# Closing rows of q from sums on VectorE and two matmuls, q's first tiles at tile 12, three modulation sums at tiles 11 to 15

## The chip, the core and the metric

The kernel runs on one core of one Trainium2 chip. The metric is the device time of one execution in microseconds (us). Five engines work beside each other: TensorE (PE in the profile, its weight loads PEld), VectorE (DVE), ScalarE (ACT), GpSimd (POOL) and SyncE (SP), which here only issues loads and stores. Each runs its own queue of instructions in the order in which the program issues them and waits on semaphores for the others.

## What is computed

The reference is a transformer block with adaptive layer norm, for 2048 tokens of width 448, all float32:

```python
mod = (_silu(c) @ w_mod).reshape(c.shape[0], 6, 1, -1)
sa, ca, ga, sb, cb, gb = (mod[:, 0], mod[:, 1], mod[:, 2], mod[:, 3], mod[:, 4], mod[:, 5])
h = _layernorm(x, axis=-1) * (1 + ca) + sa
x = x + ga * _A_ref(h, A_wqkv, A_wo)
h = _layernorm(x, axis=-1) * (1 + cb) + sb
x = x + gb * _B_ref(h, B_w1, B_b1, B_w2, B_b2)
```

`_A_ref` is linear attention with 16 heads of 28: q, k, v are `h @ wqkv`; q and k go through phi(t) = t + 1 for t > 0, else exp(t), plus 1e-6; `kv` and `z` are sums over all tokens of phi(k) v and phi(k); the output is (phi(q) kv) / (phi(q) z) times `wo`. `_B_ref` is an MLP across the tokens (2048 to 1792 and back, with GELU).

## The kernel before

Tokens are cut into 16 tiles of 128 (`NT`), channels into 4 chunks (three of 128 and one of 64). A float32 product is built from a rounded high part and a low remainder, so that one product takes three matmuls (high-high, high-low, low-high). A matmul with 448 columns is the unit of PE's work nearly everywhere.

The order of all instructions is written out by hand. The part around the change is the loop over tiles `t = 4 .. 15` (L674 to L765). One turn issues, in this order:

- **PE**: `project(t+1)`, ten matmuls of k for the next tile; `close(t)`, one matmul that adds the layer norm's mean and bias to k through "closing rows" (`Wrow`); `a_outer(t-4)`, eleven matmuls that add the tile's phi(k) times x to four banks; at odd t `a_transpose(t+1)`, which turns the means and deviations of tiles t+1 and t+2 into rows that `close` needs; and, where `Q_EARLY` says so, `a_q(i)`, the ten matmuls and the closing one of q for tile i.
- **ACT**: exponentials and ReLUs of q from the turn before (`a_exp_q`, two per tile of q); at odd t `a_copy(t+1)`, `a_copy(t+2)`, which put the transposed rows into the operand that `close` loads; `a_exp(t)` for k (at t = 9 ahead of the copies); `a_split_high(t+3)`; `a_pk_parts(t-1)`; `a_high(t-2)`.
- **DVE**: at odd t `bn_stats` of x for tiles t+3 and t+4 (the first at the start of the turn, the second late in it); `phi_q`; `a_norm`; `a_pk(t)`; `a_split_low(t+3)`; `a_low`; then at the end of the turn the sums of modulation vectors (`mod_part(j, i)`, one of four steps for vector j).
- **POOL**: the power of the variances (`a_pow`) and two accumulating DMAs per tile (`a_pk_parts`, L524, and `sum_end`, L538).
- **SP**: loads of later tiles (`FETCH`), of modulation weights (`load_mod(j)`, four loads of 196 KB) and others. Each waits for a free buffer of the pool `slots` (74 buffers of 128 x 512 float32).

Two places carry the change:

- The **closing rows of q**, `Wrow[0]`. q's weights are scaled by 1 + ca on ACT (`w_high`, tiles 4 to 7) and DVE (`w_low`, tiles 5 to 8). The rows hold minus the sum of the scaled weights over the channels and the product with sa. At t = 9, between `close(9)` and `a_outer(5)`, PE builds both: `row_sum(0)` (L290, seven matmuls of a selecting matrix `sel_s` with the high and low weights) and `row_bias(0)` (L296, one float32 matmul with `accb`, which DVE summed in `row_part`, tiles 5 to 8). `row_out(0)` (L299) rounds them into `Wrow[0]` on ACT and DVE at the end of t = 9. Tiles 0 to 4 of q follow at t = 10 to 14; the other eleven come after the loop.
- The **modulation vectors** 2 (ga), 4 (1 + cb) and 3 (sb): loaded by `load_mod`, summed in four steps on DVE, split by `mod_split`, summed over partitions by a matmul with ones (`mod_sum2`), and copied out by `mod_out`. ga multiplies the four pieces of `wo` (L764, L776).

After the loop come the last phi(k) parts, the sum `pksum`, its split `zs`, the last outer products, `zp` (L784, two matmuls of `zs` with ones), `zb` (L786), splits of the MLP's weights (`split_to`), `csum` (L795, L796) and `kvb` (L805), which PE multiplies from `csum` and v's weights.

Of the kernel before, what the change touches and what calls it, by code (L numbers as in the profile page):

```python
# [8 lines left out]
F32 = mybir.dt.float32  # L9
F32R = mybir.dt.float32r  # L10
AF = mybir.ActivationFunctionType
ALU = mybir.AluOpType
# [15 lines left out]
Q_EARLY = {10: 0, 11: 1, 12: 2, 13: 3, 14: 4}  # L28
RING = 3
FETCH = {4: 11, 5: 12, 7: 13, 9: 14, 10: 15}  # L30
# [9 lines left out]
MOD_AT = {9: [(4, 0)], 10: [(4, 1)], 11: [(4, 2)], 12: [(4, 3)], 13: [(3, 0)], 14: [(3, 1)]}  # L40
# [12 lines left out]
def block_kernel(ctx: ExitStack, tc: tile.TileContext, x, xt, wqkv, wo, w1, b1, w2, b2, c, wmod, wfirst, out):  # L53
# [63 lines left out]
    sel_s = cst.tile([P, ROWS], F32R, name="sel_s")  # L117
    rowst = []
# [19 lines left out]
    def load_mod(j):  # L138
        for k in range(4):
            wm[j, k] = (tslot if j == 5 else slot)(f"wm{j}_{k}", parts=G)  # L140
            nc.sync.dma_start(wm[j, k], wmod[k * G:(k + 1) * G, j * D:(j + 1) * D])
# [148 lines left out]
    def row_sum(j):  # L290
        rowb[j] = bank(f"rowb{j}")
        ws = [Whi[j, ch] for ch in range(4)] + [Wlo[j, ch] for ch in range(3)]
        for i, w in enumerate(ws):
            nc.tensor.matmul(rowb[j][:ROWS, :D], sel_s, w, start=(i == 0), stop=False)

    def row_bias(j):  # L296
        nc.tensor.matmul(rowb[j][:ROWS, :D], sel_b, accb.pop(j), start=False, stop=True)

# [180 lines left out]
    def a_q(t):  # L479
        project(t, 0, "qp")  # L480
        qps[t] = close(t, 0)
        del heads[t]
# [138 lines left out]
    load_mod(2)  # L621
# [51 lines left out]
    late = [t for t in range(NT) if t not in Q_EARLY.values()]  # L673
    for t in range(4, NT):  # L674
# [3 lines left out]
        if t == 9:  # L678
            row_sum(0)
            row_bias(0)  # L680
# [4 lines left out]
        if t in Q_EARLY:  # L685
            a_q(Q_EARLY[t])
        if t == 12:
            mp = mod_sum2(2)
# [10 lines left out]
        a_phi_q(t in Q_EARLY)  # L699
        if t == 9:  # L700
            a_exp(t, kp)
# [3 lines left out]
        if t != 9:  # L705
            a_exp(t, kp)
# [29 lines left out]
        if t == 9:  # L736
            row_out(0)
        if t == 12:
            mod_out(2, mp)
            make_mask()  # L740
# [3 lines left out]
        if 7 <= t < 11:  # L744
            mod_part(2, t - 7)
        if t == 11:
            mod_split(2)
        for j, i in MOD_AT.get(t, ()):
            mod_part(j, i)
        if t in (7, 10):  # L750
            load_mod(4 if t == 7 else 3)
# [11 lines left out]
        if t >= 13:  # L763
            nc.vector.tensor_mul(wo_sb[t - 13], wo_sb[t - 13], mods[2][:G])  # L764
# [11 lines left out]
    nc.vector.tensor_mul(wo_sb[3], wo_sb[3], mods[2][:G])  # L776
# [587 lines left out]
```

## Time and profile before

| what | us |
|---|---|
| median of 3 runs (lowest, highest) | 436.17 (435.62, 436.36) |
| the profiled execution | 435.4 |
| its span in the profile | 433.7 |
| the granted clock of PE, all 40 slices | 0.9 or more of full speed |

The profile is one execution on the chip. Times in it count from the span's start. A view named "timeline" lists instructions of an engine: start, duration, engine, line, operation, output and inputs, and in brackets the idle time before it with what ended it. The "chain of waits" follows the last instruction back to what released it, step by step, so that its rows together fill the span. The "waits" list who waited for whom: total, times, longest. Successive matmuls overlap: a 448-column matmul lasts 0.36 us in the list, and the next one starts about 0.20 us after it, so PE's cost is read from starts.

### The profile page before, as it was taken

How to read it: one execution, taken by the hardware profiler on the slowest of the kernel's cores; microseconds unless marked ns; L12 is line 12 of the kernel's file. 1: busy time of each engine (PE TensorE's matmuls, PEld its weight loads, DVE VectorE, ACT ScalarE, POOL GpSimd, SP SyncE). 2: the span in 40 equal slices, each digit the busy share in tenths (PEclk: the TensorE clock that was granted, in tenths of full speed). 3: DMA queues.
4: the chain of work that ended last, by engine and by line, in shares of the span. 5: the costliest groups of instructions: out<-in, count | busy, mean ns of one | idle time of the engine just before them, and what ended most of it. 6: DMA issues, size and time to landing. Idle time of an engine off the chain costs nothing.

```text
span 433.7 us, 7208 instructions
## 1 busy us (share of the span) xinstructions
PE 428.1 (99%) x2333; PEld 395.5 (91%) x2333; DVE 362.2 (84%) x813; ACT 278.5 (64%) x595; POOL 119.6 (28%) x198
## 2 busy tenths in 40 slices
PE   8999999999999999999999999999999999999996
PEld 7788899999899989989999999999999999999996
DVE  4999987689799999996579695739799998898893
ACT  5899868658578799985855263537464664645550
POOL 2336444300025577775200000010113131122010
PEclk9999999999999999999999999999999999999999
DMA  8998996574200036345427461587479977886430
GB/s 278 384 334 179 242 249 152 107 225 164 86 1 0 26 73 148 73 98 121 147 85 241 144 212 50 167 209 201 85 181 215 228 157 153 218 176 125 82 54 32
DMA packets 63941, 66.14 MB, mean 152 GB/s; under 512 B 4960, under 2 KB 55456, under 8 KB 63904
## 3 DMA queue, kind: packets, MB, share of 16 engines
q1 hardware_dynamic: 54832, 50.90, 37.8%
q0 software_dynamic: 8784, 14.32, 21.1%
q10 hardware_dynamic: 288, 0.46, 0.5%
q8 instruction: 18, 0.29, 0.3%
q14 instruction: 19, 0.16, 0.1%
HBM read 46.30 MB, written 7.34 MB: 124 GB/s over the span
## 4 chain that ended last, share of the span: by engine, by line
PE 92%; DVE 4%; DMA 2%; issue 0%; POOL 0%; ACT 0%; SPq 0%; DVEq 0%
PE y L1159 19%; PE up L939 10%; PE up L938 10%; PE up L940 10%; PE y L1160 9%; PE cacc L551 8%; PE qp L439 7%; PE op L881 6%; PE kp L439 5%; PE tq L851 1%; PE op L888 1%; DMA wr<-in_qkv_dram 1%; DMA xt<-in_xt_dram 1%; PE qp L446 1%; PE kvb L805 1%; PE wp L955 1%
## 5 line engine op out<-in xcount | busy, mean ns | idle before, releaser
L939 PE MATMUL up<-h2l,ph 128*128 128x448 f32 x224 | 81.3, 363 | 0.0
L938 PE MATMUL up<-h2h,ph 128*128 128x448 f32 x224 | 81.2, 362 | 0.0
L940 PE MATMUL up<-h2h,pl 128*128 128x448 f32 x224 | 80.8, 361 | 0.0
L1114 POOL DMA_DIRECT2D a<-a x16 | 14.2, 962 | 137.8 <-DMA a<-in_B_w_dram 77.6
L938 PEld LDWEIGHTS up<-h2h,ph 128*128 128x128 f32 x224 | 42.0, 188 | 3.2
L940 PEld LDWEIGHTS up<-h2h,pl 128*128 128x128 f32 x224 | 41.9, 187 | 3.0
L939 PEld LDWEIGHTS up<-h2l,ph 128*128 128x128 f32 x224 | 42.0, 188 | 2.6 <-DVE h2l L935 0.3
L85 DVE TENSOR_TENSOR pl<-pr,ph 128x512 fp32r<-128x512 f32 x46 | 30.8, 688 | 4.1 <-ACT ph L84 3.3
L1165 ACT ACTIVATE cc<-y 128x448 f32<-128x448 f32 x24 | 13.0, 546 | 26.8 <-PE y L1160 26.8
L84 ACT ACTIVATE ph<-pr 128x512 fp32r<-128x512 f32 x46 | 27.6, 623 | 0.8 <-PE up L940 0.5
L1078 DVE TENSOR_TENSOR u<-u,mod 128x448 f32<-128x448 f32 x14 | 8.7, 623 | 21.7 <-ACT u L1077 21.5
L1077 ACT ACTIVATE u<-up,b1c 128x448 f32<-128x448 f32 x14 | 8.8, 625 | 24.1 <-PE up L940 23.5
L1179 POOL DMA_DIRECT2D out_dram<-yt x14 | 12.7, 908 | 40.8 <-DVE yt L1170 31.4
L439 PE MATMUL kp<-wh,hh 128*128 128x448 f32 x64 | 23.7, 375 | 0.0
L551 PE MATMUL cacc<-pkh,xh 128*128 128x448 f32 x64 | 23.6, 369 | 0.0
L439 PE MATMUL qp<-wh,hh 128*128 128x448 f32 x64 | 23.4, 366 | 0.0
L831 POOL TENSOR_SCALAR den<-den 128x16 f32<-128x16 f32 x16 | 8.8, 549 | 45.4 <-DVE den L828 45.4
L551 PE MATMUL cacc<-pkl,xh 128*128 128x448 f32 x56 | 20.3, 362 | 0.0
L881 PE MATMUL op<-wph,pth 128*128 128x448 f32 x48 | 18.7, 390 | 0.0
L1120 DVE TENSOR_TENSOR a<-a,s 128x512 f32<-128x512 f32 (+1 forms) x32 | 18.5, 622 | 0.0
L84 ACT ACTIVATE s2h<-s 128x512 fp32r<-128x512 f32 (+1 forms) x16 | 8.3, 569 | 15.5 <-DVE s L1120 15.5
L1159 PE MATMUL y<-ub,a11h 128*128 128x448 f32 x56 | 18.2, 375 | 0.0
(239 smaller groups left out, 1378.1 us busy)
## 6 DMA issues: line engine op xcount, KB each, us to landing
pr<-in_B_w_dram SPq DMA_DIRECT2D x56, 256.0 KB, 3.1
a<-in_B_w_dram SPq DMA_DIRECT2D x32, 256.0 KB, 4.4
a<-in_B_w_dram SPq DMA_DIRECT2D x32, 192.0 KB, 4.2
xt<-in_xt_dram SPq DMA_DIRECT2D x16, 256.0 KB, 5.0
x<-in_A_x_dram SPq DMA_DIRECT2D x16, 224.0 KB, 5.0
wm<-in_B_wmod_dram SPq DMA_DIRECT2D x16, 196.0 KB, 5.4
out_dram<-x SPq DMA_DIRECT2D x14, 224.0 KB, 2.2
out_dram<-yt POOLq DMA_DIRECT2D x14, 224.0 KB, 5.7
```

The source lines that it names most:

```text
L84: nc.scalar.activation(hi, full, AF.Copy)
L85: nc.vector.tensor_sub(lo, full, hi.bitcast(F32))
L439: nc.tensor.matmul(pps[t, j][:, :D], a[:, ch * P:(ch + 1) * P], w, start=first, stop=False)
L551: nc.tensor.matmul(cacc[ch][:, :D], a[:, s], b, start=(t == 0 and i == 0), stop=(t == NT - 1 and i == len(todo) - 1))
L881: nc.tensor.matmul(opb[t][:, :D], a, b, start=(ch == n == 0), stop=False)
L938: nc.tensor.matmul(ps[:, :D], hi[:, sl], mh, start=first, stop=False)
L939: nc.tensor.matmul(ps[:, :D], hi[:, sl], ml, start=False, stop=False)
L940: nc.tensor.matmul(ps[:, :D], lo[:, sl], mh, start=False, stop=last)
L1114: nc.gpsimd.dma_start(w, a, accum_op=ALU.add)
L1120: nc.vector.tensor_tensor(w, raw2[q, a][i], raw2[q, b][i], op=op)
L1159: nc.tensor.matmul(ps[:, :D], h[:, s], w, start=opens and r == 0, stop=False, skip_group_check=True)
L1160: nc.tensor.matmul(ps[:, :HD], l[:, s], wh, start=False, stop=closes and r == PAIRS - 1, skip_group_check=True)
```

## The change

q's closing rows are no longer built by eight matmuls at t = 9. DVE sums the scaled weights over the four chunks into one tile `accs` (`row_main`: chunks 0 and 1 at t = 9, chunks 2 and 3 at t = 10). `row_fold` (end of t = 10) adds the two halves of the partitions, of this sum and of `accb`, into the two halves of one tile. `row_cut` (t = 11, ahead of the turn's copies) splits it, on ACT and DVE. `row_both` (t = 12, after `close(12)`) multiplies the high and low part with a new selecting matrix `sel_q`, two matmuls, and `row_out(0)` follows at once. `sel_q` is made by `make_sel_q` at the end of t = 8: seven memsets on POOL and a rounding copy on ACT.

Tiles 0 to 4 of q move from t = 10 .. 14 to t = 12 (two), 13, 14 and 15. The first loads of modulation weights move from ahead of the loop to t = 7 (vector 2), and from t = 7 and 10 to t = 9 (4) and 11 (3). The sums move from t = 7 .. 14 to t = 11 .. 15; the split of vector 2 from t = 11 to 13, its matmul and copy (and the mask's memset) from t = 12 to 14; the products of `wo` from t = 13, 14, 15 and one after the loop to two at t = 15 and two after it. At t = 9, `a_exp` goes behind the copies as at other odd tiles.

```diff
-Q_EARLY = {10: 0, 11: 1, 12: 2, 13: 3, 14: 4}
+Q_EARLY = {12: (0, 1), 13: (2,), 14: (3,), 15: (4,)}
+ROW_AT = 12
+MAIN_AT = {9: (0, 1), 10: (2, 3)}
+MOD2_AT = {11: (0,), 12: (1, 2, 3)}
 RING = 3
+LOAD_MOD = {7: 2, 9: 4, 11: 3}
...
-MOD_AT = {9: [(4, 0)], 10: [(4, 1)], 11: [(4, 2)], 12: [(4, 3)], 13: [(3, 0)], 14: [(3, 1)]}
+MOD_AT = {13: [(4, 0), (4, 1)], 14: [(4, 2), (4, 3)], 15: [(3, 0), (3, 1)]}
...
+    def make_sel_q():
+        g = slot("sel_g", P)
+        nc.gpsimd.memset(g, 0.0)
+        for i in (64, 66, 96):
+            nc.gpsimd.memset(g[:64, i:i + 1], -1.0)
+            nc.gpsimd.memset(g[64:, i + 1:i + 2], 1.0)
+        nc.scalar.activation(sel_q, g, AF.Copy)
+
+    def row_main(j, ch):
+        p = slice(0, P) if ch < 3 else slice(0, 64)
+        if ch == 0:
+            accs[j] = slot(f"accs{j}")
+            nc.vector.tensor_scalar_mul(accs[j], raw_w[j, 0], col[1][:, 0:1])
+        else:
+            nc.vector.scalar_tensor_tensor(accs[j][p], raw_w[j, ch][p], col[1][p, ch:ch + 1], accs[j][p],
+                                           op0=ALU.mult, op1=ALU.add)
+
+    def row_fold(j):
+        s, b = accs[j], accb.pop(j)
+        nc.vector.tensor_add(s[:64], s[:64], s[64:])
+        nc.vector.tensor_add(s[64:], b[64:], b[:64])
+
+    def row_cut(j):
+        s = accs.pop(j)
+        hi, lo = moving(slot, f"rfh{j}"), moving(slot, f"rfl{j}")
+        nc.scalar.activation(hi, s, AF.Copy)
+        nc.vector.tensor_sub(lo, s, hi.bitcast(F32))
+        accs[j] = (hi, lo)
+
+    def row_both(j):
+        rowb[j] = bank(f"rowb{j}")
+        for i, m in enumerate(accs.pop(j)):
+            nc.tensor.matmul(rowb[j][:ROWS, :D], sel_q[:, :ROWS], m, start=(i == 0), stop=(i == 1))
...
-    load_mod(2)
...
-        if t == 9:
-            row_sum(0)
-            row_bias(0)
+        if t == ROW_AT:
+            row_both(0)
+            row_out(0)
...
-        if t in Q_EARLY:
-            a_q(Q_EARLY[t])
-        if t == 12:
+        for i in Q_EARLY.get(t, ()):
+            a_q(i)
+        if t == 14:
             mp = mod_sum2(2)
...
-        a_phi_q(t in Q_EARLY)
-        if t == 9:
-            a_exp(t, kp)
+        a_phi_q(len(Q_EARLY.get(t, ())))
+        if t == ROW_AT - 1:
+            row_cut(0)
...
-        if t != 9:
-            a_exp(t, kp)
+        a_exp(t, kp)
...
-        if t == 9:
-            row_out(0)
-        if t == 12:
+        for ch in MAIN_AT.get(t, ()):
+            row_main(0, ch)
+        if t == ROW_AT - 2:
+            row_fold(0)
+        if t == 8:
+            make_sel_q()
+        if t == 14:
             mod_out(2, mp)
             make_mask()
...
-        if 7 <= t < 11:
-            mod_part(2, t - 7)
-        if t == 11:
+        for i in MOD2_AT.get(t, ()):
+            mod_part(2, i)
+        if t == 13:
             mod_split(2)
...
-        if t in (7, 10):
-            load_mod(4 if t == 7 else 3)
+        if t in LOAD_MOD:
+            load_mod(LOAD_MOD[t])
...
-        if t >= 13:
-            nc.vector.tensor_mul(wo_sb[t - 13], wo_sb[t - 13], mods[2][:G])
+        if t == 15:
+            for w in wo_sb[:2]:
+                nc.vector.tensor_mul(w, w, mods[2][:G])
...
-    nc.vector.tensor_mul(wo_sb[3], wo_sb[3], mods[2][:G])
+    for w in wo_sb[2:]:
+        nc.vector.tensor_mul(w, w, mods[2][:G])
```

More of the change, by code (lines that the diff above doesn't have):

```diff
@@ L117, in block_kernel @@
     sel_s = cst.tile([P, ROWS], F32R, name="sel_s")
+    sel_q = cst.tile([P, P], F32R, name="sel_q")
     rowst = []
@@ L297, in row_bias @@
         nc.tensor.matmul(rowb[j][:ROWS, :D], sel_b, accb.pop(j), start=False, stop=True)
+    accs = {}
+    def make_sel_q():
[27 more added lines that the diff above has]
+            nc.tensor.matmul(rowb[j][:ROWS, :D], sel_q[:, :ROWS], m, start=(i == 0), stop=(i == 1))
     def row_out(j):
@@ L672, in block_kernel @@
     wo_sb = []
-    late = [t for t in range(NT) if t not in Q_EARLY.values()]
+    late = [t for t in range(NT) if t not in sum(Q_EARLY.values(), ())]
     for t in range(4, NT):
```

## The prediction

> **What bounds the kernel now.** I read the page's first part, then the windows, then the chain of waits around t = 9, then the timelines of the queues there.
>
> ```profile
> PE 428.1 (99%) x2333; PEld 395.5 (91%) x2333; DVE 362.2 (84%) x813; ACT 278.5 (64%) x595; POOL 119.6 (28%) x198
> ```
>
> ```profile
> 40.00:50.00 10.00, 10.00 (x51) 8.87 (x50) 9.82 (x26) 9.84 (x21) 6.12 (x7) 1.00 0.99 208
> ...
> 60.00:70.00 10.00, 10.00 (x53) 9.31 (x52) 7.09 (x17) 4.85 (x11) 3.05 (x4) 1.00 1.01 258
> ```
>
> PE is busy nearly the whole span, at full clock (1.00 in the windows), so a matmul less is time less, and a stall of PE is time more. But DVE and ACT (9.82 and 9.84 of 10 us) are as full as PE between 40 and 50 us, and have room only from 60 us on (7.09 and 4.85), where q's tiles stretch each turn on PE.
>
> ```profile
> 48.50 1.42 PE rowb L294 x7
> 49.92 0.75 PE rowb L297 x2
> 50.67 2.21 PE cacc L551 x11
> ...
> 57.41 2.00 PE qp L439 x10
> ```
>
> In the chain (start, us, what) the matmuls of the closing rows stand on PE from 48.50 to 50.67, with nothing beside them. Ten matmuls take 2.00 us, so one takes 0.20. A turn without q takes 2.00 + 0.20 + 2.21 = 4.41 us, a tile of q adds 2.20.
>
> **The change part by part.**
>
> *PE.* The chain loses 2.17 us (48.50 to 50.67) and gains two matmuls, 0.41: **-1.76 us**. q's matmuls only move. Bounds: -1.76, and -1.0 if only the seven matmuls' 1.42 were saved and the float32 matmul's stretch came back as another gap. I take the whole stretch, since the chain shows it as PE's own time.
>
> *Turns 9 to 12.* When PE would need things without a stall: from 48.50, `a_outer(5)` and the transposition 2.32, turn 10 4.41, turn 11 4.52, `project(13)` and `close(12)` 2.20, the two new matmuls 0.41, `a_outer(8)` 2.21, `project` of q's tile 0 2.00, so its closing matmul, which needs the new rows, is due at 66.6. `close(10)` is due at 52.8, `close(12)` at 61.8. Turns 10 and 11 lose q's 2.20 each: DVE and ACT lose that room. First comes the new wait, for `sel_q`. ACT and POOL as they stand:
>
> ```profile
> 50.08 0.62 ACT L453 ACTIVATE ek<-kp,mv 128x448 f32<-128x448 f32 x1
> 50.60 0.63 ACT L456 ACTIVATE rk<-kp,mv 128x448 f32<-128x448 f32 x1
> 53.03 0.57 ACT L414 ACTIVATE hl<-rw 34x128 fp32r<-34x128 f32 x2 [1.81 <-PE rw L411]
> ```
>
> ```profile
> 50.11 0.86 POOL L524 DMA_DIRECT2D pkl<-pk  x1 [0.47 <-ACT pkl L523]
> 51.63 0.86 POOL L538 DMA_DIRECT2D pk<-pk  x1 [0.66 <-DVE xl L509]
> ...
> 74.90 1.24 POOL L538 DMA_DIRECT2D pk<-pk  x1
> 75.43 1.19 POOL L97 MEMSET mask<- 112x448 f32 x1
> ```
>
> ```profile
> 1.43 0.18 POOL L113 MEMSET sel_f<- 128x98 f32 x1
> 1.67 0.10 POOL L115 MEMSET sel_f<- 128x1 f32 x1
> ```
>
> ```profile
> L559 ACT ACTIVATE sel_s<-sel_f x1: 270/270/270, 2.6 to 2.6; 128x98 fp32r<-128x98 f32 x1
> ```
>
> The copy of `sel_q` is the last of turn 8 on ACT, where the `ek` of 50.08 started before. Its seven memsets stand on POOL behind the DMA of 51.63, the last of turn 8. POOL goes on 0.53 after such a DMA starts (74.90, 75.43), so the memsets run from 52.2 for 0.18 + 6 x 0.10, and ACT's copy of 0.27 ends at about **53.2**. Behind it on ACT are queued `a_copy(10)`, `a_copy(11)` and turn 9's exponentials. `close(10)` waits for the first copy, until 53.5 instead of 52.8.
>
> Then DVE, in its own order, with durations like these (the next start counts, not the end):
>
> ```profile
> 48.45 0.69 DVE L287 SCALAR_TENSOR_TENSOR accb<-wr,col,accb 128x448 f32<-128x448 f32 x1
> ...
> 51.36 0.68 DVE L233 SCALAR_TENSOR_TENSOR acc<-wm,sc,acc 112x448 f32<-112x448 f32 x1
> ...
> 65.95 0.63 DVE L461 SCALAR_TENSOR_TENSOR pk<-ek,rk 128x448 f32<-128x448 f32 x1 [2.17 <-ACT rk L456]
> ```
>
> So 0.60 for each step of a sum, 0.53 for a phi. Let S = 53.2. On ACT two copies take 0.58, `ek` and `rk` 1.15: rk9 is there at S + 1.75; with `hh`, `pkh`, `pkl`, `xh` (2.1 more) xh7 is there at S + 3.85. DVE has pk9, hl12 and a `bn_stats` (1.73), a wait for xh7, `a_low(7)` 0.60, the pair's end 0.25, two `row_main` 1.05: S + 5.8. Turn 10 has norm, rows, pk, hl and low, 2.5, two `row_main` 1.2, `row_fold` twice 0.53: **S + 10.6**. Only then can ACT cut the sum (0.57), and `a_copy(12)` is queued behind the cut: `close(12)` can start at S + 11.5 = 64.7 instead of 61.8. ACT then has the second copy and two exponentials (S + 12.95), DVE pk11, hl14, a `bn_stats`, a wait for xh9 (S + 15.0), `a_low(9)` 0.60, the pair's end 0.25, the first step of vector 2 0.45 and at last `row_out`'s subtraction, a little over 0.6: S + 16.95 = **70.15, against 66.6: +3.5 us**, the two stalls before it included.
>
> Bounds. If DVE never waited: the removed first step of vector 2 began at 47.25, from there turns 8 to 11 hold 3.6, 4.9, 4.6 and 5.0 us and the subtraction 0.6, which ends at 66.0: stall 0. If `sel_q` were no wait, S would be the end of the transposition, 51.05: +1.45. If x15's load comes late (below): +5.4. I take +3.5: each wait in it stands behind a row above.
>
> [...]
>
> ```profile
> 57.52 0.69 DVE L233 SCALAR_TENSOR_TENSOR acc<-wm,sc,acc 112x448 f32<-112x448 f32 x1
> ```
>
> ```profile
> 56.91 1.03 POOL L359 TENSOR_TENSOR mv<-ve,roots 128x4 f32<-128x4 f32 x1 [0.29 <-DVE ve L393]
> ```
>
> *Turns 13 to 15 and after.* DVE gets here what left turns 7 to 11.
>
> ```profile
> 77.43 0.27 PE L411 MATMUL rw<-ident,rowst 128*98 128x128 f32 x1
> ...
> 97.82 0.36 PE L784 MATMUL zp<-zl,ones_r 128*128 128x448 f32 x1
> ```
>
> ```profile
> 79.52 0.63 DVE L461 SCALAR_TENSOR_TENSOR pk<-ek,rk 128x448 f32<-128x448 f32 x1 [2.54 <-ACT rk L456]
> ...
> 96.23 0.62 DVE L85 TENSOR_TENSOR zl<-pk,zh 128x448 fp32r<-128x448 f32 x1 [0.70 <-ACT zh L84]
> ...
> 102.10 2.47 DVE L796 SCALAR_TENSOR_TENSOR cs<-zb,col,cs 128x448 f32<-128x448 f32 x4
> ```
>
> ```profile
> PEld kvb L805 <- DVE cs L796: 0.2, 1, 0.2
> ```
>
> From turn 13's transposition (77.43) DVE, which waits for it through ACT, needs 19.4 us to the end of `zl` (96.85), and PE 20.4 to the matmul that takes it: 1.0 to spare. The change puts six modulation steps in place of two there (+2.2), the split of vector 2 (+1.1) and two products of `wo` in place of three (-0.5): +2.7 busy, and up to +3.4 with ACT's hop inside the split and its added copies. PE gets one more tile of q and the sum of vector 2: +2.4. So 0.0 to 0.7 us are left at `zl`. Behind it, q's fifth phi and one more product of `wo` (0.54 + 0.53) come ahead of `cs`, for which PE's `kvb` waited already (0.2). The stall at `kvb` is 1.07 + (0.3 to 1.0) = 1.4 to 2.1; I take **+1.8**, the middle, as the waits of 2.54 and 0.70 may swallow a part. Bounds: 0, if the waits in between swallow all of it, and 2.5, if ACT's two exponentials of q's fifth tile (50.08 to 51.2 for such a pair) hold up its phi too.
>
> *At nothing.* The loads of vectors 2, 4 and 3 stand four turns, over 17 us, ahead of their first use, which covers them. The mask's three operations on POOL are due only at `kvb`; without that cover they would cost their 2.7 us or so. The same holds for the copy of vector 2 on ACT, due at t = 15. On SP, turn 9's four loads now stand ahead of turn 10's load of tile 15, and five tiles of q hold two buffers each for longer: a rival.
>
> **Sum.** -1.76 + 3.5 + 1.8 = +3.5 us, on the profiled execution of 435.4 us, which lies 0.8 under the median of 436.17. On the median: **439.7 us**.
>
> **The rivals.**
> - *`sel_q` is no wait* (POOL reaches its memsets early): -1.76 + 1.45 + 1.8 = +1.5, **437.7**. For it: POOL stood idle 0.66 before 51.63. Against it: ACT reaches the copy at 50.1, and POOL's DMA of 50.11 alone ends later.
> - *DVE keeps up* (the faster side): relieved of its sums in turns 7 to 11, it runs with hardly a wait and ends `row_out` by 66.6 and `cs` at most 0.3 late: -1.76 + 0.3, **434.7**. It decides at `row_fold`: ended by 60.9, there is no stall. For it: 66.0 of bare work. Against it: 0.6 us of waits use that up, and single waits of 2.17 and 2.54 stand above.
> - *A load comes late*: x15, for the second `bn_stats` of t = 11, waits on SP for a buffer that POOL's accumulating DMA of t = 9 frees. SP had such a wait:
>
> ```profile
> SPq L141 <- DMA pk<-pk: 3.0, 1, 3.0
> ```
>
> ```profile
> x<-in_A_x_dram SPq DMA_DIRECT2D x16, 224.0 KB, 5.0
> ...
> pk<-pk POOLq DMA_DIRECT2D x11, 224.0 KB, 4.9
> ```
>
>   That DMA would be issued at about 59.5, land 4.9 later, the load 5.0 after that, 69.4 against S + 14.1 = 67.3; the wait for xh9 hides 0.3: +1.8, **441.5**.
> [...]
> - *Balance*: half of the stalls are absorbed by waits that shrink elsewhere, -1.76 + 2.0: **436.4**.
>
> **How the numbers follow.** Forecast 0.39, `sel_q` no wait 0.18, DVE keeps up 0.24, late load 0.07, port lock 0.02, balance 0.10. A measurement of this kernel can tell about 0.2% (0.87 us) from no change. Slower by more: 0.39 + 0.18 + 0.07 + 0.02, less 0.02 of the second case that falls within: 0.64. Faster 0.24, within 0.12. The range goes from 434.6, which leaves out a little under half of the faster case, to 441.8, above which only the worst ends of the unknown costs lie. The forecast's own range is 438 to 441.
>
> **What would show it.** Right: in the changed kernel's trace ACT stands idle before the copies of t = 9, released by POOL; PE waits at `close(10)`, `close(12)` and q's first closing matmul, 3.5 us together; PE at `kvb` waits 1 to 2 us for `cs`. Wrong: no wait of PE between 50 and 72 us, `row_fold` ended by 60.9, or `kvb` no later behind `zp` than before (5 us).

## The result, and the profile after

The changed kernel takes 446.21 us (median of 4 runs, 445.24 to 449.22), the kernel before 435.89 us beside it (4 runs): a ratio of 1.0252, interval 1.0208 to 1.0295, 10.3 us slower. The forecast was 439.7, the range ended at 441.8. The profiled execution took 446.08 us, its span 444.4, 10.7 more than the span of 433.7 before.

The first part of its page (engine, busy time, share, instructions):

```profile
PE 432.4 (97%) x2326; PEld 399.4 (90%) x2326; DVE 367.4 (83%) x820; ACT 279.2 (63%) x597; POOL 119.9 (27%) x205
```

Seven matmuls fewer, and yet 4.3 us more busy: at a lower clock each matmul takes longer (the ten from 67.60 on start within 3.73 us, where ten took 2.00 before). The windows of 10 us show the clock (busy time of PE, PEld, DVE, ACT, POOL, then the granted clock, the DMA share, GB/s):

```profile
60.00:70.00 10.00, 7.72 (x34) 6.54 (x34) 8.82 (x21) 5.96 (x13) 4.13 (x5) 0.89 0.97 215
...
110.00:120.00 10.00, 8.13 (x48) 7.66 (x48) 8.86 (x16) 6.16 (x12) 0.00 (x0) 0.83 0.25 80
```

PE has waits where it stood at 10.00 before, and the clock is under 1.00 in two places, where it was 1.00 throughout. PE's timeline shows the stalls (start, duration, what, then the idle time before it and what ended it):

```profile
48.80 0.37 PE L592 MATMUL cacc<-pkh,xh 128*128 128x448 f32 x1
50.76 0.47 PE L592 MATMUL cacc<-pkl,xh 128*128 128x448 f32 x1 [1.59 <-DMA pkl<-pk]
...
56.07 0.47 PE L487 MATMUL kp<-wrow,hl 98*128 98x448 f32 x1 [0.90 <-ACT hl L455]
...
67.60 0.56 PE L487 MATMUL kp<-wrow,hl 98*128 98x448 f32 x1 [2.28 <-ACT hl L455]
...
111.93 5.02 PE L850 MATMUL kvb<-cs,wr 128*112 128x112 f32 x32 [1.87 <-DVE cs L841]
116.72 0.45 PE L265 MATMUL modp<-mh,ones_r 112*128 112x448 f32 x1
```

Matmuls start 0.20 us apart where nothing waits, so what lies between two starts beyond that is a loss: 50.76 - 48.80 - 0.20 = 1.76 for the first. Where the 10.7 us are, with the starts of the matmuls on both sides:

| | forecast | measured |
|---|---|---|
| rows' eight matmuls gone, two added | -1.76 | -1.76 |
| a_outer(5) waits for pkl (48.80 to 50.76) | 0 | +1.76 |
| close(10) (54.80 to 56.07) and close(12) (64.96 to 67.60) | +3.5, with q's first close | +1.07 + 2.44 = 3.51 |
| ten starts from 67.60 to 71.33 in 3.73 instead of 2.0 | 0 | +1.73 |
| five small gaps from 101.4 to 109.6 | in the next | +0.9 |
| kvb (109.59 to 111.93) | +1.8 | +2.14 |
| kvb's matmuls, 4.79 to the next instead of 3.17 | 0 | +1.62 |
| sum | +3.5 | +9.9 |

Some 0.5 of the 0.8 us left arose before 48 us (`project(10)` starts at 46.59 instead of 46.14). The two rows with the slow starts are the low clock. Windows laid on its edges show it:

```profile
47.35:50.76 3.41, 1.82 (x11) 1.35 (x9) 2.85 (x9) 3.24 (x7) 2.31 (x2) 1.00 1.17 227
64.42:67.83 3.41, 1.13 (x6) 0.69 (x4) 3.24 (x7) 1.11 (x3) 0.08 (x1) 1.00 1.07 235
67.83:71.24 3.41, 3.41 (x10) 2.95 (x10) 2.10 (x5) 3.33 (x8) 0.22 (x1) 0.50 1.06 309
71.24:74.65 3.41, 3.41 (x18) 3.17 (x18) 2.51 (x8) 2.63 (x6) 2.68 (x3) 1.00 0.94 164
108.79:112.20 3.41, 1.48 (x7) 0.80 (x6) 3.41 (x7) 3.41 (x8) 0.00 (x0) 1.00 0.02 5
112.20:115.61 3.41, 3.41 (x21) 3.41 (x20) 3.41 (x7) 3.41 (x8) 0.00 (x0) 0.50 0.28 80
```

The length of 3.41 us is that of the two stretches at 0.50 in this trace, 67.83 to 71.24 and 112.20 to 115.61; between them lie 40.96 us at 1.00, twelve times as long. After a window of 3.41 us in which PE was busy for 1.13 or 1.48 us, the next window runs at half clock; after the one with 1.82 it does not. Such a window need not be idle as a whole: 1.9 us of idleness in one were enough here.

Upstream, the wait for `sel_q` is there, but later than forecast. ACT, then POOL:

```profile
55.41 0.31 ACT L312 ACTIVATE sel_q<-sel_g 128x128 fp32r<-128x128 f32 x1 [4.79 <-POOL sel_g L311]
```

```profile
41.90 0.86 POOL L565 DMA_DIRECT2D pkl<-pk  x1 [0.18 <-issue]
43.95 0.86 POOL L579 DMA_DIRECT2D pk<-pk  x1 [1.19 <-DVE st L428]
47.76 0.88 POOL L565 DMA_DIRECT2D pkl<-pk  x1 [2.95 <-ACT wh L272]
...
54.04 0.54 POOL L308 MEMSET sel_g<- 128x128 f32 x1
```

The DMA of 41.90, tile 5's, is the one that `a_outer(5)` waits for. A line of the view of that one instruction, after, and below it the same line of its counterpart before:

```profile
DMA to landing us min/median/max: 8.8/8.8/8.8
```

```profile
DMA to landing us min/median/max: 6.1/6.1/6.1
```

What had changed there is SP's queue. After, and before:

```profile
38.52 2.18 SPq L146 DMA_DIRECT2D wm<-in_B_wmod_dram  x4
40.75 3.09 SPq L800 DMA_DIRECT2D wo<-in_A_wo_dram  x4
```

```profile
40.15 5.33 SPq L141 DMA_DIRECT2D wm<-in_B_wmod_dram  x4
45.53 3.05 SPq L757 DMA_DIRECT2D wo<-in_A_wo_dram  x4
```

Before, SP waited for buffers in the middle of vector 4's loads, and so `wo`'s came at 45.5. Vector 2's, moved to t = 7, find buffers at once, and eight loads of 196 KB go out within 5.3 us, just when POOL's accumulating DMAs are on their way.

### The profile page after: what moved, and what is told of

Its sections match the earlier page's. It is cut to its first block, busy times and chain, and to the rows that moved or that the text cites. A ratio compares the mean times of both kernels' runs of the same rounds, so it can differ in the third digit from the quotient of the medians.

```text
span 444.4 us, 7209 instructions
## 1 busy us (share of the span) xinstructions
PE 432.4 (97%) x2326; PEld 399.4 (90%) x2326; DVE 367.4 (83%) x820; ACT 279.2 (63%) x597; POOL 119.9 (27%) x205
## 4 chain that ended last, share of the span: by engine, by line
PE 76%; DVE 9%; DMA 7%; ACT 4%; issue 2%; POOL 2%; SPq 0%; POOLq 0%; ACTq 0%; DVEq 0%
PE y L1204 18%; PE up L985 10%; PE up L984 10%; PE up L983 10%; PE y L1205 9%; PE op L926 6%; PE qp L480 5%; DMA xt<-in_xt_dram 2%; DMA wr<-in_qkv_dram 2%; PE cacc L592 2%; PE tq L896 1%; PE op L933 1%; DMA pk<-pk 1%; PE kvb L850 1%; DMA pr<-in_B_w_dram 1%
## 5 line engine op out<-in xcount | busy, mean ns | idle before, releaser
L1204 PE MATMUL y<-ub,a12h 128*128 128x448 f32 x56 | 18.2, 374 | 0.0
```

The costliest lines, as they stand in the source:

```text
L1204: nc.tensor.matmul(ps[:, :D], h[:, s], w, start=opens and r == 0, stop=False, skip_group_check=True)
```

## The experiments

Eighteen kernels ran, each with the kernel before on the same chip. Its median was 435.4 to 436.0 us every time. The ratio is estimated from the single executions and differs a little from the quotient of the medians. A trace shows one execution.

| kernel | median us | ratio to before (interval) |
|---|---|---|
| changed | 446.21 | 1.0252 (1.0208 to 1.0295) |
| sel_early | 445.39 | 1.0209 (1.0185 to 1.0232) |
| loads_old | 444.32 | 1.0202 (1.0182 to 1.0221) |
| sel_loads | 444.16 | 1.0197 (1.0182 to 1.0212) |
| slots76 | 442.10 | 1.0154 (1.0120 to 1.0187) |
| sel_loads_own | 441.92 | 1.0141 (1.0126 to 1.0156) |
| after_nosum (leaves work out) | 446.82 | 1.0253 (1.0236 to 1.0271) |
| mods_alone | 440.52 | 1.0107 (1.0092 to 1.0122) |
| q_alone | 437.20 | 1.0037 (1.0023 to 1.0051) |
| rows_q | 442.12 | 1.0147 (1.0130 to 1.0164) |
| rows_10 | 439.26 | 1.0080 (1.0063 to 1.0097) |
| cut_behind | 442.81 | 1.0167 (1.0153 to 1.0182) |
| cut_light | 439.85 | 1.0094 (1.0080 to 1.0108) |
| cut_light_own | 439.56 | 1.0098 (1.0081 to 1.0115) |
| light_nosum (leaves work out) | 438.10 | 1.0047 (1.0032 to 1.0062) |
| stall10, 12 | 438.17, 439.26 | 1.0051, 1.0076 (each within 0.0017) |
| stall14, 16 | 441.33, 442.59 | 1.0133, 1.0158 (each within 0.0018) |

### The wait for sel_q, and the loads

sel_early is the changed kernel with

```diff
+    sel_g = cst.tile([P, P], F32, name="sel_g")
+    nc.gpsimd.memset(sel_g, 0.0)
+    for i in (64, 66, 96):
...
     def make_sel_q():
-        g = slot("sel_g", P)
-        nc.gpsimd.memset(g, 0.0)
...
-        nc.scalar.activation(sel_q, g, AF.Copy)
+        nc.scalar.activation(sel_q, sel_g, AF.Copy)
```

> The changed kernel, with the seven memsets for sel_q made at the start of the kernel instead of at the end of turn 8; ACT's copy stays where it is. Theory A (the waits of turns 9 to 12 start at the copy of sel_q, which ACT reached at 50.6 us and which waited 4.8 us for POOL): ACT no longer waits there, a_copy(10) runs right behind its transposition (53.2 instead of 55.7), the wait of 0.9 us at close(10) goes, the chain of DVE to row_cut ends 2.5 us sooner, close(12) waits about 1.1 instead of 2.3 us, and with less than half of a clock window idle the clock stays at 1.00 there: about 1.1 + 1.3 + 1.7 = 4.1 us less, 442 us. Theory B (DVE and ACT are simply too full in turns 9 to 12, sel_q only shows where the wait ends): close(12) waits as long as before, the clock falls as before, under 1.2 us less, 445 us or more. The wait of 1.6 us at a_outer(5) stays under both.

Theory A fell. The wait for POOL went, close(10) no longer stalled, and the median fell by 0.8 us, less than the intervals can tell from nothing. ACT's timeline in sel_early:

```profile
59.75 0.64 ACT L494 ACTIVATE ek<-kp,mv 128x448 f32<-128x448 f32 x1 [2.48 <-DMA pk<-pk]
...
66.42 0.58 ACT L331 ACTIVATE rfh<-accs 128x448 fp32r<-128x448 f32 x1 [3.44 <-DVE accs L326]
```

The copy starts 2.3 us sooner, but turn 10's exponential then waits for the landing of a DMA of POOL's, whose source buffer it takes over, and the cut starts at 66.42 instead of 66.67. close(12) waits 2.9 us, and the low clock is there (0.93 in the mean from 60 to 70 us).

loads_old moves the loads alone:

```diff
-LOAD_MOD = {7: 2, 9: 4, 11: 3}
+LOAD_MOD = {9: 4, 11: 3}
...
     load_x(9)
+    load_mod(2)
...
-        if t == 8:
+        if t == 9:
             for g in range(4):
                 w = tslot(f"wo{g}", parts=G)
```

> The changed kernel, with the loads of vector 2 back at their old place (ahead of tile 10's loads) and the loads of wo and the two biases one turn later (t = 9), so that SP issues nothing big between 38.5 and 45 us. Theory A (these loads share the DMA engines with POOL's accumulating DMAs; the DMA of pkl of tile 5 took 8.8 us to land instead of 6.1, and POOL, which never had more than three DMAs out, issued each next one 0.3 us after the oldest had landed, up to 2 us later than before): that DMA lands in 6 us or less, the wait of 1.6 us at a_outer(5) goes, POOL's memsets for sel_q come some 2 us sooner; PE is then sooner too by 1.8 us, so the stalls at close(10) and close(12) and the low clock stay about as they were: 1.5 to 2.5 us less, about 444 us. Theory C (the late landing has another cause, such as POOL's own order): the wait at a_outer(5) stays, no gain.

As theory A has it: the median is 1.9 us less. (The intervals of the changed kernel and loads_old still overlap, so it is the trace that decides.) Tile 5's DMA landed 4.0 us after its issue at 41.3, `a_outer(5)` waits for nothing, and ACT's copy of `sel_q` starts at 52.86, so that it ends at 53.2, where the forecast had it:

```profile
52.86 0.31 ACT L312 ACTIVATE sel_q<-sel_g 128x128 fp32r<-128x128 f32 x1 [2.87 <-POOL sel_g L311]
```

So the moved loads made both the wait at `a_outer(5)` and the error of 2.5 us in S. close(10) and close(12) still wait 0.8 and 2.3 us, and q's first close now waits 1.0. sel_loads has both edits.

> The changed kernel with both edits: sel_q's memsets at the start of the kernel, vector 2's loads at their old place, those of wo and the biases at t = 9. Theory A: the gains add up and the chain behind close(10) starts from the transposition: 1.8 (a_outer(5)) + 1.1 (close(10)) + 1.5 (close(12)) + 1.7 (clock) = 6 us less, 440 us; what is left over 436.2 is the wait at kvb with its low clock, 1.9 + 1.7 us and some small waits. Theory B: 443 us or more.

It gained 2.0 us on the changed kernel, hardly more than the loads alone. PE's longest wait in it (engine, tile and line, what ended it, then us in total, times, longest):

```profile
PE kp L487 <- ACT hl L455: 3.2, 1, 3.2
```

What was taken from two waits came back in one, at close(12).

### The buffers behind POOL's DMAs

slots76 has one edit on sel_loads, which turns the order in which buffers are handed out; sel_loads_own gives the tiles that POOL's accumulating DMAs read six buffers of their own instead and leaves 70 for the rest, so it too has 76 in all.

```diff
-NSLOT, NTOK = 74, 27
+NSLOT, NTOK = 76, 27
```

```diff
+    pkp = ctx.enter_context(tc.tile_pool(name="pkp", bufs=6))
...
-        pkf[t] = phi_k(t, ps, tslot if t < 2 else slot)
+        pkf[t] = phi_k(t, ps, tslot if t < 2 else slot if t < 4 else pslot)
```

> sel_loads with 76 buffers in the pool of slots instead of 74, which turns the order in which they are handed out: the first exponential of turn 10 no longer takes the buffer that POOL's accumulating DMA of tile 7 reads (ACT waited 2.8 us for that landing in sel_loads), tile 15's load no longer that of tile 8. Theory E (with sel_q's wait gone, that buffer is the next wait; behind it DVE would have room): the wait of ACT goes, row_fold ends 1.5 to 2.5 us sooner, close(12) waits 1 to 2 instead of 3.2 us and the clock stays at 1.00 there: 3 to 4.5 us less than sel_loads, about 440.5 us. Theory B (DVE and ACT are too full for turns of 4.4 us without q): close(12) still waits 2.5 us or more and the clock falls, 443 us or more.

> sel_loads (sel_q's memsets at the start, vector 2's loads at their old place, wo's at t = 9) with six buffers of their own for the phi(k) tiles that POOL's accumulating DMAs read, and 70 for the rest. Theory J (those landings, 5 to 7 us after the issue, hand on the buffers for which ACT, DVE and SP wait in turns 9 to 12): no engine waits for a landing of such a DMA there, the chain to row_fold is 1.5 to 2.5 us sooner than in sel_loads, close(12) waits 1 to 2 us instead of 3.2, the clock mostly stays: 444.2 - 1.5 to 4 = 440 to 442.5 us. Theory B (DVE's own work): as sel_loads, 443.5 us or more.

slots76 got half of what theory E expected: the exponential's wait went, and ACT's split of tile 13 waited 2.2 us instead; close(12) still waited 2.6. (The trace is of its slowest execution, 444.09; two others took 441.1.) With buffers of their own no wait for such a landing is left in turns 9 to 12, close(12) waits 0.9 us, the clock stays at 1.00 there (it falls only behind kvb), and 2.2 us are gained on sel_loads: theory J by the waits. By the time alone it could as well be the two buffers more: slots76 gained 2.1 with them, and the two intervals overlap. A kernel with 74 in all and six set apart was not run. Two of PE's waits in sel_loads_own:

```profile
PE qp L491 <- DVE wrow L347: 1.5, 1, 1.5
...
PE kp L491 <- ACT hl L459: 0.9, 1, 0.9
```

The 1.5 us at q's first close are the third stall of the forecast's chain; in the changed kernel the first two and the low clock probably covered it.

### The parts alone

mods_alone and q_alone each put one part of the change into the kernel before.

```diff
-MOD_AT = {9: [(4, 0)], 10: [(4, 1)], 11: [(4, 2)], 12: [(4, 3)], 13: [(3, 0)], 14: [(3, 1)]}
+MOD_AT = {13: [(4, 0), (4, 1)], 14: [(4, 2), (4, 3)], 15: [(3, 0), (3, 1)]}
+MOD2_AT = {11: (0,), 12: (1, 2, 3)}
...
-        if t == 11:
+        if t == 13:
             mod_split(2)
...
```

```diff
-Q_EARLY = {10: 0, 11: 1, 12: 2, 13: 3, 14: 4}
+Q_EARLY = {12: (0, 1), 13: (2,), 14: (3,), 15: (4,)}
...
```

> The kernel before, with only the sums of vectors 2, 4 and 3, the split and the matmul of vector 2 and the products of wo moved to where the change has them; rows, q and all loads stay as they were. Theory A (DVE's work moved into turns 13 to 15 makes cs late for kvb, and a wait of PE of about 2 us also costs a clock window at half speed, 1.7 us): kvb waits 1.5 to 3 us for cs, the clock falls to 0.5 for 3.4 us there, 2 to 4.7 us more than the kernel before, 438 to 441 us. Theory D (the wait at kvb comes from the fifth tile of q ahead of it, not from the sums): no wait at kvb over 0.7 us, 436 to 437 us.

> The kernel before, with only the first five tiles of q moved from turns 10 to 14 to where the change has them (two at 12, then one each until 15); the rows' eight matmuls stay at t = 9, sums and loads where they were. Theory B (q's 2.2 us in turns 10 and 11 gave DVE, ACT and POOL the time that they need; turns of 4.4 us are too short for them): close(12) waits 1 to 3 us for its copy though there is neither sel_q nor a chain through row_fold, 1.5 to 5 us more than the kernel before, 437.5 to 441 us. Theory F (only the new chain, row_fold and its cut ahead of a_copy(12), holds close(12) up): no wait over 0.5 us there, and at most the fifth phi ahead of cs at kvb, 0.5 to 1 us: 436.5 to 437 us.

The sums alone cost 4.7 us, at the top of what was expected, but not as expected: kvb waits 1.2 us, three matmul groups before it 1.2, 0.4 and 0.2, and the clock stays at 1.00. PE's first two waits in mods_alone:

```profile
PE cacc L552 <- DVE pkl L522: 1.2, 1, 1.2
PE kvb L808 <- DVE cs L799: 1.2, 1, 1.2
```

q alone costs 1.7 us, and not at close(12), where PE waits for nothing: it waits 1.4 us for vector 2's bank, which is wanted beside q's two. So turns without q are not too short by themselves; theory F, not B.

rows_q leaves the sums and their loads as before and has sel_q's memsets early; rows_10 also moves the rows' sum to t = 7 and 8, so that q can stay at tiles 10 to 14, and vector 2's sum to t = 9 to 11.

```diff
-MOD2_AT = {11: (0,), 12: (1, 2, 3)}
+MOD2_AT = {7: (0,), 8: (1,), 9: (2,), 10: (3,)}
...
-MOD_AT = {13: [(4, 0), (4, 1)], 14: [(4, 2), (4, 3)], 15: [(3, 0), (3, 1)]}
+MOD_AT = {9: [(4, 0)], 10: [(4, 1)], 11: [(4, 2)], 12: [(4, 3)], 13: [(3, 0)], 14: [(3, 1)]}
...
```

```diff
-Q_EARLY = {12: (0, 1), 13: (2,), 14: (3,), 15: (4,)}
+Q_EARLY = {10: (0,), 11: (1,), 12: (2,), 13: (3,), 14: (4,)}
...
-ROW_AT = 12
-MAIN_AT = {9: (0, 1), 10: (2, 3)}
-MOD2_AT = {7: (0,), 8: (1,), 9: (2,), 10: (3,)}
+ROW_AT = 10
+MAIN_AT = {7: (0,), 8: (1, 2, 3)}
+MOD2_AT = {9: (0,), 10: (1, 2), 11: (3,)}
```

> The change without its moved sums: rows from VectorE's sums at tiles 9 to 11 and q from tile 12 on, sel_q's memsets at the start; the sums of vectors 2, 4 and 3, the products of wo and all modulation loads as in the kernel before. If the moved sums cost at kvb and the small waits before it what they cost alone (4.7 us in mods_alone; 2.9 us of waits and 1.7 of clock in the changed kernel), and DVE's steps of vectors 2 and 4 come back into turns 7 to 11 (2.3 us ahead of row_fold): kvb waits under 0.7 us, close(12) 1 to 2 us longer than in sel_early, 441 to 443 us. If kvb's wait comes from q's fifth tile instead: kvb still waits over 1.2 us, 444 us or more.

> Rows from VectorE's sums two turns sooner (steps at t = 7 and 8, the fold at 8, the cut at 9, the two matmuls at 10), so that q stays at tiles 10 to 14 as in the kernel before; vector 2's sum two turns later (t = 9 to 11), the other sums, products and loads as before; sel_q's memsets at the start. PE saves 1.8 us and keeps q in turns 10 and 11. If DVE takes the 2.2 us net in turns 7 to 9 without a stall: 434.5 us, under both kernels. If it can't (9.8 of 10 us busy from 10 to 50 us): close(10) waits for the cut that stands ahead of its copy, 1 to 3 us, and 1.7 us of clock if the wait passes about 2 us: 435.5 to 439 us. I expect the second.

rows_q's time is as expected, rows_10's just over. In rows_q the wait at kvb is gone, and close(12) waits 3.2 us, only 0.3 more than in sel_early where 1 to 2 were expected. rows_q is q_alone with the rows changed, and 4.9 us slower: these rows cost more than the 1.8 us of PE that they save. In rows_10 the stall sits at close(10), with 2.9 us and a low clock (0.996 in the mean of the execution): it goes wherever the cut stands.

### The order of ACT's queue, or DVE's work

cut_behind takes rows_q and lets nothing queue behind the cut.

```diff
-        if t == ROW_AT - 1:
-            row_cut(0)
         if t % 2 and 4 < t < NT - 2:
             a_copy(t + 1)
             a_copy(t + 2)
         a_exp(t, kp)
+        if t == ROW_AT - 1:
+            row_cut(0)
...
+        if t == ROW_AT:
+            project(0, 0, "qp")
+            row_both(0)
+            row_out(0)
+            project(1, 0, "qp")
+            for i in (0, 1):
+                qps[i] = close(i, 0)
```

> rows_q with nothing queued behind the wait for row_fold: ACT's cut of the sum stands behind the two copies and the exponentials of turn 11 instead of ahead of them, and at t = 12 PE goes close(12), a_outer(8), q0's ten matmuls, the two new matmuls, q1's ten, and then the two closing matmuls of q; vector 2's matmul one turn later (13), so that its bank is not wanted beside q's two. Theory G (the place of the cut in ACT's queue makes the stall at close(12), not the amount of work): close(12) waits under 0.7 us, no low clock between 60 and 75 us, at most 1 us of waits at the new matmuls or q's closes: 442.1 - 3.3 - 0.9 - 1.7 - 1.0 = 435 to 437 us, level with the kernel before. Theory B (DVE and ACT too full without q in turns 10 and 11, whatever stands where): close(12) or the matmuls behind it wait 2 us or more in sum, 439 us or more.

cut_light also moves DVE's other sums out of its way (vector 2's split too, from t = 11 to 12), and cut_light_own gives it the six buffers of sel_loads_own.

```diff
-MOD2_AT = {7: (0,), 8: (1,), 9: (2,), 10: (3,)}
+MOD2_AT = {7: (0,), 8: (1,), 10: (2,), 11: (3,)}
...
-MOD_AT = {9: [(4, 0)], 10: [(4, 1)], 11: [(4, 2)], 12: [(4, 3)], 13: [(3, 0)], 14: [(3, 1)]}
+MOD_AT = {12: [(4, 0), (4, 1)], 13: [(4, 2), (4, 3)], 14: [(3, 0)], 15: [(3, 1)]}
...
```

> cut_behind with DVE's load moved out of turns 9 to 11 in part: vector 2's last two steps at t = 10 and 11 (behind row_fold) instead of 9 and 10, vector 4's four steps at t = 12 and 13 instead of 9 to 12, vector 3's first two at 14 and 15. Theory G: DVE reaches row_fold some 1.1 us sooner, the waits left in turns 10 to 12 (1.1 us at the transposition in rows_q among them) go; kvb waits at most 1 us: 433.5 to 436 us, at or under the kernel before. Theory B: as cut_behind, 438 us or more.

> cut_light (nothing queued behind the cut, DVE lighter in turns 9 to 11, sums not in turn 15 and after) with six buffers of their own for the same tiles. Theory J: DVE and ACT are no longer held up for 2.1 and 0.75 us by a landing, the wait of 3.2 us at q's second tile is under 1 us and the clock stays at 1.00: 439.9 - 2.5 - 1.7 = 435.5 us, level with the kernel before or a little under. Theory B: 438 us or more.

Theory G was right that close(12) stalls where the cut stands: it waits for nothing in all three. But the matmuls behind it wait 5.6, 3.2 and 1.8 us, and the times are those that theory B expected; theory J's 435.5 was not reached. q's second tile now waits for a bank, which turn 12's exponentials have to free; they stand on ACT behind work that waits in its turn, in cut_behind 2.7 us for a sum of DVE's, in cut_light 1.2 for DVE's norm, in cut_light_own 1.7 for the rows' two matmuls. One row of each kernel, cut_behind, cut_light, cut_light_own:

```profile
PE qp L480 <- ACT rk L497: 5.6, 1, 5.6
```

```profile
PE qp L480 <- ACT rk L497: 3.2, 1, 3.2
```

```profile
PE qp L484 <- ACT rk L501: 1.8, 1, 1.8
```

Relief for DVE and then for the buffers each shrinks it, but the second gained no time: the intervals of cut_light and cut_light_own overlap. What is left of 4 us over the kernel before is spread in cut_light_own: besides this wait 0.6 us for a landing, 1.0 at kvb and some smaller ones; the traced execution, 438.9, had full clock, the other three (439.5 to 440.3), by their mean clock of 0.996, a window at half clock.

Two kernels leave three of the four steps of the rows' sum and both additions out, after_nosum of the changed kernel and light_nosum of cut_light.

```diff
-        for ch in MAIN_AT.get(t, ()):
-            row_main(0, ch)
+        if t == 9:
+            row_main(0, 0)
...
-        nc.vector.tensor_add(s[:64], s[:64], s[64:])
-        nc.vector.tensor_add(s[64:], b[64:], b[:64])
```

> The changed kernel without VectorE's work for the rows' sum: it leaves out three of the four steps of row_main and both additions of row_fold (3.0 us of DVE in turns 9 and 10), so the rows' sums are not computed; every wait, copy, matmul and load stays in its place, sel_q's too. If the work is what makes close(12) late: ACT's cut waits for nothing, close(12) waits under 0.5 us, the clock stays at 1.00 behind it: 446.2 - 2.4 - 1.7 = 442 us. If sel_q and POOL's late DMAs make it late by themselves: close(12) still waits 1.5 us or more, 444 us or more.

> cut_light with the same work left out (three steps of row_main and both additions of row_fold). If the work of DVE is the cause of the wait of 3.2 us at q's second tile: DVE is 3 us ahead, that wait is under 0.5 us and the clock stays: 439.9 - 3.2 - 1.7 = 435 us. If the eight banks or the order of ACT's queue is: the wait stays at 1.5 us or more, 437.5 us or more.

after_nosum answers both halves of the question with one surprise. close(12) stalls no more: the work is what made it late. And nothing is gained. PE's first waits in it, then ACT's row:

```profile
PE qp L485 <- DVE wrow L341: 3.5, 1, 3.5
PE kvb L848 <- DVE cs L839: 1.9, 1, 1.9
```

```profile
67.35 0.63 ACT L457 ACTIVATE hh<-xt 128x512 fp32r<-128x512 f32 x1 [2.99 <-issue]
```

The row does not name what the split of tile 14 waited for. POOL's DMA of 61.08 took 6.2 us and landed at 67.28, just ahead of it, so the split probably takes the buffer that this DMA reads. Behind the split, q's first close waits 3.5 us. The clock then stays at 0.50 for two windows, 6.8 us, instead of one, and does not fall behind kvb, so the time at half clock is the same in sum.

light_nosum comes to 438.1, and the wait at q's second tile stays at 1.8 us: the second expectation. PE, then ACT there:

```profile
66.38 0.36 PE L336 MATMUL rowb<-rfl,sel_q 128*98 128x448 f32 x1
68.56 0.48 PE L478 MATMUL qp<-wh,hh 128*128 128x448 f32 x1 [1.81 <-ACT rk L495]
```

```profile
66.78 0.54 ACT L340 ACTIVATE wrow<-rowb 34x448 fp32r<-34x448 f32 x1 [2.55 <-PE rowb L336]
67.34 0.63 ACT L492 ACTIVATE ek<-kp,mv 128x448 f32<-128x448 f32 x1
67.88 0.63 ACT L495 ACTIVATE rk<-kp,mv 128x448 f32<-128x448 f32 x1
```

Here the order makes the wait. Turn 12's exponentials, which free the bank, are queued on ACT behind `row_out`, which needs the two new matmuls, and these stand on PE right ahead of q's second tile. So some 1.8 us of this wait in cut_behind, cut_light and cut_light_own would stay if DVE were never late. The work, the buffers and the order each make a wait in these turns, and one hides the other; what each costs by itself is not shown.

### What a stall costs

These are the kernel before with a stall made on purpose at one place, n copies on ACT ahead of `a_copy(12)`:

```diff
+    dum = cst.tile([P, D], F32, name="dum")
...
+        if t == 11:
+            for _ in range(14):
+                nc.scalar.activation(dum, X[9], AF.Copy)
         if t % 2 and 4 < t < NT - 2:
             a_copy(t + 1)
```

> The kernel before, with 14 copies of 128 x 448 on ACT ahead of a_copy(12) in turn 11, into a tile that nothing reads: a stall of PE made on purpose, with nothing of the change. ACT is free there from 60.8 us, a copy takes 0.60 start to start, close(12) is due at 68.3: the copy that it waits for ends at about 69.8, PE waits 1.5 us. Theory H (a stall costs its own length while it fills less than half of a clock window of 3.41 us, and 1.7 us more, a window at half clock, when it fills more than about 55%): no low clock, 1.5 us more than the kernel before, 437 to 437.8 us. Theory I (the low clock in the changed kernel has another cause than the stall, such as the load of all engines): no low clock either here or in the next kernel.

> The same with 16 copies: PE waits 2.7 us at close(12). Theory H: the clock falls to 0.5 for a window of 3.41 us behind the stall in executions where the window's grid puts 1.9 us or more of the stall into one window (in most), 2.7 + 1.7 = 4.4 us more than the kernel before, 439.5 to 440.5 us. Theory I: 2.7 us more, 438.2 us, and no low clock.

> The kernel before with 10 copies on ACT ahead of a_copy(12), four fewer than in stall14, where PE waited 3.5 us: PE waits 3.5 - 4 x 0.61 = 1.1 us. Theory H: no low clock, 1.2 to 1.4 us more than the kernel before, 436.6 to 436.9 us.

> The same with 12 copies: PE waits 2.3 us. Theory H: where the grid of windows puts at least 1.9 us of the wait into one window of 3.41 us, a window at half clock follows: 2.4 + 1.7 = 4.1 us more, 439.6 us; where it is cut in two, 2.4 us more, 437.9 us. If only an idle window as a whole lowers the clock: 437.9 us always.

The first two waited 3.5 and 4.7 us, 2 us longer than meant, since it is `project(13)`, 2.0 us ahead of close(12), that needs the copies first. They cost 5.9 and 7.2 us. stall10 waits 1.1 us, the clock stays at 1.00, and it costs 2.2, 0.8 over the expectation; a second wait of 0.5 is a part of that, the rest is not assigned. stall12 waits 2.3 us, and pays for the clock in its profiled execution, 3.9 us of span; its median is 3.3 over. Its windows:

```profile
65.72:69.13 3.41, 1.13 (x6) 0.72 (x6) 0.00 (x0) 3.24 (x8) 0.00 (x0) 1.00 0.84 275
69.13:72.54 3.41, 3.41 (x11) 3.03 (x10) 2.67 (x7) 2.41 (x5) 0.87 (x1) 0.50 0.01 2
```

Nothing but the stall differs from the kernel before, so the low clock comes from the stall: theory I falls, and theory H holds for the traces. For the whole time it holds less well. One window at half clock takes 0.004 off an execution's mean clock (0.996 in stall12's trace with one, 0.988 in that of sel_loads with three). stall12's three other executions had 0.999, as many of the kernel before have, so no such window, and took 438.9 to 439.4 all the same, where theory H has 437.9; in rows_10 the two without it were the slower ones (439.6 against 438.5 and 439.0). In q_alone the one execution with it (0.996) took 438.7, the seven others 436.5 to 437.6. What the executions without it lost instead, no trace shows.

One wait that met the edge of a window got off: in loads_old kvb waits the same 1.9 us, but they fall into two windows with 2.02 and 2.86 us of busy PE, and the clock stays:

```profile
107.30:110.73 3.43, 2.02 (x9) 1.30 (x7) 3.43 (x7) 3.43 (x7) 0.00 (x0) 1.00 0.01 3
110.73:114.14 3.41, 2.86 (x29) 2.86 (x30) 3.41 (x7) 3.41 (x8) 0.00 (x0) 1.00 0.20 56
```

No kernel here beats the one before.

## Why the prediction was wrong

Its sign was right, its size not: +3.5 forecast, +10.3 measured. The signs that were to show it right came nearly all: ACT idle before the copies of t = 9 until POOL was done, PE waiting at close(10) and close(12), 1.9 us at kvb; only q's first close did not wait. They could not show what had been put at nothing. By its own steps:

- **PE -1.76**: right, and at once given back. a_outer(5) starts 1.9 us sooner than before and waits 1.6 for tile 5's DMA.
- **"At nothing"**: this step failed. It asked whether the moved loads would be there in time, and they were. It did not ask what they would hold up: POOL's DMA of tile 5 took 2.7 us longer to land, POOL's later work moved back with it, and S came at 55.7 instead of 53.2. loads_old, with the loads put back, has S at 53.2 and no wait at a_outer(5).
- **S + 10.6 to row_fold, S + 11.5 to close(12)**: counted from the S that came about, 66.3 and 67.2; measured 66.6 and 67.6. The two stalls of close(10) and close(12) sum to 3.51, the forecast 3.5. That is partly luck: the forecast had 2.9 for these two and the rest at q's first close, which did not wait, and S came 2.5 us late, but PE came to close(10) 2.2 late itself (55.0 instead of 52.8), mostly through a_outer(5). The agreement proves less than it seems for another reason: sel_early took the start of the chain away and the median fell by 0.8 us, where the prediction's rival "`sel_q` is no wait" priced that at 2.0. A second chain, through buffers behind POOL's DMAs, ended almost at the same time.
- **Each stall at its own length**: the other step that failed. Two of the stalls were also followed by a window at half clock, 1.73 and 1.62 us in this trace. The stall kernels show such windows without anything of the change, though not that every execution pays for them in its total.
- **kvb +1.8**: the mechanism was right, the term too small. Measured 2.14 at kvb and 0.9 in the small gaps before it; mods_alone has 4.7 for the sums alone, above the bound of 2.5. The waits that were taken to swallow a part swallowed little: of the two, the one of 2.54 shrank to 1.35, the one of 0.70 stayed at 0.71, and a new one of 0.65 came inside the split of vector 2. From turn 13's transposition to the end of `zl` DVE took 23.3 us instead of 19.4, 3.9 more, where 2.7 to 3.4 were forecast, and behind it q's fifth phi waited 0.42 for ACT, which only the upper bound had.
- **Rivals**: "DVE keeps up" was to be decided at row_fold, ended by 60.9; it ended at 66.6. The "port lock" of the chances was priced as a wait of DVE for POOL's power, +1.0, and no run shows that term. Before, the sum of 57.52 started while the power of 56.91 ran (both rows stand in the prediction) and took 0.69; after, in the next rows, the step of 60.97 ran inside POOL's power and took 0.69 too, and the power 1.10. What the traces do show is a difference on POOL's side. Over the twenty traces (kernel before, changed, and the eighteen), the 120 powers that started while DVE ran a step with two SBUF inputs took 1.31 to 1.75 us; of the 40 others 38 took 1.03 to 1.18 (two 1.70 and 1.82), though times on POOL are rough in this profile. What makes the difference was not tested. Tile 15 was loaded before DVE came to it; the late load did not decide.

```profile
60.97 0.69 DVE L320 SCALAR_TENSOR_TENSOR accs<-wr,col,accs 128x448 f32<-128x448 f32 x1
```

```profile
60.73 1.10 POOL L400 TENSOR_TENSOR mv<-ve,roots 128x4 f32<-128x4 f32 x1 [0.36 <-DVE ve L434]
```

The missing 7.2 us of span are a_outer(5) with 1.76, the clock with 3.35, kvb and its neighbours with 1.26, and 0.8 that was not assigned. What stays open: which of the remaining small waits would have to go for these rows to pay. The best version with them, rows_10, is 0.8% behind the kernel before.

## What to carry to other kernels

A transfer that is moved is to be priced twice: whether it arrives in time, and what else is on its way when it goes out earlier (here tile 5's DMA, 8.8 us to its landing instead of 6.1). In these twenty traces the clock stayed where PE was idle for at most 1.72 us of a window of 3.41; after 1.80 or more a window at half clock followed, which cost 1.73 and 1.62 us in the changed kernel; the total did not always grow by as much (stall12, rows_10). Where several queues are nearly full over the same stretch, one chain timed well gives the time that you will see, but not what you get for removing its first wait: look for the second chain, and among others for buffers that a slow DMA hands on (2.48 us of ACT's time in sel_early).

## What the runs showed of the hardware

- **The clock's window.** Over the twenty traces, nineteen windows at full clock were followed by half clock; PE was busy in them for 0.00 to 1.61 of 3.41 us. The lowest that was not so followed had 1.69, so in these traces the line lies between the two, a little under half of the window. These two, of light_nosum and of cut_light_own:

```profile
66.57:69.99 3.42, 1.61 (x8) 1.36 (x8) 2.91 (x8) 3.15 (x6) 0.21 (x1) 1.00 1.06 301
69.99:73.40 3.41, 3.41 (x11) 2.95 (x10) 3.32 (x9) 0.69 (x2) 3.41 (x4) 0.50 0.35 74
```

```profile
68.22:71.63 3.41, 1.69 (x8) 1.59 (x9) 2.79 (x7) 3.35 (x7) 2.10 (x2) 1.00 1.10 295
71.63:75.04 3.41, 3.41 (x18) 3.17 (x18) 2.31 (x5) 1.96 (x5) 1.77 (x2) 1.00 0.70 118
```

To come back took more: five windows at half clock with PE busy for 0.19 to 2.69 us were followed by a second one, the nineteen with 3.28 or more by full clock. In sel_loads 2.26 us did not suffice, and its one stall of 3.2 us was followed by 6.8 us at half clock:

```profile
60.31:63.72 3.41, 1.40 (x7) 0.96 (x6) 3.07 (x6) 0.21 (x1) 1.72 (x2) 1.00 1.15 273
63.72:67.13 3.41, 2.26 (x6) 2.02 (x7) 2.55 (x6) 3.10 (x7) 0.00 (x0) 0.50 1.11 268
67.13:70.55 3.42, 3.42 (x10) 3.03 (x10) 3.11 (x8) 1.74 (x4) 1.95 (x2) 0.50 1.06 343
```

- **POOL had never more than three DMAs on their way**, in any of the twenty traces. In the changed kernel the DMA of 40.82 took 6.6 us to land, at 47.4, and the next was issued at 47.76; that of 41.90 landed at 50.7, the next came at 51.02; that of 43.95 at 52.0, the next at 52.30. So these late landings moved everything behind them on POOL, memsets too: the first for `sel_q` started at 54.04, where the forecast had 52.2. Why there were never more than three was not tested.
